# Attention as two 64-row phases with swapped row tiles, single score units between, up heads in the last chunk only

## The chip, the cores and the metric

The kernel runs on one core of one Trainium2 chip. The metric is device time in microseconds, the median of several runs; lower is better.

## The reference

Two stages follow each other. A gated attention without softmax, for eight batches of 3008 rows, 256 columns and 64 columns of z, and then a feed-forward over all 24064 rows:

```python
scores = scale * np.matmul(z, z.transpose(0, 2, 1))   # scale = 1/S, S = 3008
attn = np.maximum(scores, 0.0) ** 2
x = u * np.matmul(attn, v)                            # per batch, [3008, 256]
h = x.reshape(B * S, D) @ w_in                        # d_ff = 2048
g = h * (1.0 / (1.0 + np.exp(-1.702 * h)))
out = g @ w_out
```

Scores are symmetric, since z meets itself.

## The kernel before

**Tiles.** A batch of 3008 rows is 23 blocks of 128 rows and one block of 64; six chunks of 512 columns (the last of 448) are the columns of attention. Everything runs in float16 with float32 sums. ZT holds z transposed, and holds it twice: in partitions 0-63 and again in 64-127.

**Scores.** `scores` (L188) makes a unit: two blocks j of rows for one chunk i. The contraction is over 64 values, so its two matmuls (L198) use the upper and the lower 64 rows of TensorE at once, each into its own PSUM bank of one `sc` tile. ScalarE takes relu and scale out of PSUM (L210, L207), VectorE squares (L224, L215, L208) into an `a` tile. Because of the symmetry a block computed for chunk i also serves, transposed by a DMA on SP's queue (L217, L230: `ad`, `tt`), a later chunk. `take` (L410) pulls the next few units from a fixed list in a planned step of the program; the tables `SCHED`, `SCHED0` (batch 0) and `TAIL` say how many at which step. All units of one `take` issue their matmuls first.

**Attention.** `attend` (L252) makes one chunk's list of steps. For each half c of the 256 columns it sums over j into one PSUM bank `o` (L281), with v (`V`) as the stationary operand, and `a` or `tt` as the moving one. The 23 full blocks use all 128 rows of TensorE; the block of 64 rows is one step (`None`) that runs both halves c at once, one in the upper and one in the lower 64 rows. The halves c follow each other: 23 steps for c = 0, 23 for c = 1, with the half step between or at a place that `AT` or `AT0` gives. In batch 0, chunks 0 and 1, both c run side by side (`both`). At the end of each c `gate` (L286) multiplies the sum by u, transposed, into `xt` on VectorE.

**u.** `load_u` (L161) issues four DMAs from POOL's queue (L168) into one of two `uq` buffers, `turn_u` (L171) transposes on VectorE (L175). In the loop both are issued at the step that `TURN` names, step 12 in most chunks: chunk i of batches 1-7 turns the u of chunk i + 1 and loads that of chunk i + 3 where there is one, batch 0 turns its own chunk i and loads chunk i + 2.

**Feed-forward.** `up_group` (L307) makes two blocks of d_ff for one chunk (L314: `hg`, four matmuls), with the activation on ScalarE (L322) and a scale on VectorE (L323). `down` (L328) makes eight matmuls `yp` of 256 columns (L337), and on every fourth call ScalarE empties the bank (L343) and may issue the output's DMA (L349). The first `LAGY` = 19 up groups of a batch stand between the attention steps of chunks 4 and 5, as `HEAD` says (heads). After attention the rest alternate with `down`; then the last 17 or 19 `down` calls (the tail) carry the first twelve score units of the next batch.

**Buffers and order.** PSUM has two pools: `ps2`, three tiles of two banks (`sc`, `hg`, and `zp` at the start), and `ps1`, two tiles of one bank (`o`, `yp`). All engines run in the written order (`manual_schedule`), so each engine's queue is the order of the Python calls.

```python
for n, step in enumerate(attend(b, i, b == 0 and i < 2, half_at.get(i, 0))):
    ...
    take(b, sched[i].get(n, 0))
    h0, hn = head_at.get(i, (n + 1, 1))
    if head < LAGY and n >= h0 and (n - h0) % hn == 0:
        up_group(b, head)
        head += 1
    step()
```

Of the kernel before, what the change touches and what calls it, by code (L numbers as in the profile page):

```python
# [9 lines left out]
F32 = mybir.dt.float32  # L10
F16 = mybir.dt.float16
P = 128
# [3 lines left out]
def kernel(  # L16
# [20 lines left out]
    NJ = (S + P - 1) // P  # L37
    S0 = (S // P) * P
    SREM = S - S0
    CH = 512  # L40
    NCH = (S + CH - 1) // CH
    CB = CH // P
# [13 lines left out]
    dve, act, pe, sp, pool = nc.vector, nc.scalar, nc.tensor, nc.sync, nc.gpsimd  # L56
# [6 lines left out]
    pu = ctx.enter_context(tc.tile_pool(name="pu", bufs=2))  # L63
    pa = ctx.enter_context(tc.tile_pool(name="pa", bufs=1))
    pw = ctx.enter_context(tc.tile_pool(name="pw", bufs=2))
    ps2 = ctx.enter_context(tc.tile_pool(name="ps2", bufs=3, space=bass.MemoryType.PSUM))
    ps1 = ctx.enter_context(tc.tile_pool(name="ps1", bufs=2, space=bass.MemoryType.PSUM))
    ET = mybir.EngineType
    ctx.enter_context(tc.manual_schedule(engines={ET.PE, ET.Pool, ET.SP, ET.DVE, ET.Activation}))

# [3 lines left out]
    dve.memset(nil, 0.0)  # L74

    ZT, V16, UQ, UT, XT, unit, TT = {}, {}, {}, {}, {}, {}, {}

    def warm_up(n):

        w = ps1.tile([P, CH], F32, name="w", tag="ps1")  # L80
        for k in range(n):
            pe.matmul(w, nil[:, :P], nil, start=(k == 0), stop=(k == n - 1))
# [27 lines left out]

    def first_zt(g):
        z2 = ZT["st"][:, g * CB:(g + 1) * CB]
        zp = ps2.tile([P, CB, P], F16, name="zp", tag="ps2")
        for k in range(CB):
            pe.transpose(zp[:, k, :], z2[:, k, :, :], ident)  # L115
        zt = ZT[0][:, g * CB:(g + 1) * CB, :].rearrange("d n p -> d (n p)")
        nb = CB if g < NCH - 1 else CB - 1
        dst = zt[:, :nb * P].rearrange("d (p n) -> d n p", n=nb)
        if g == 0:
            act.activation(dst, zp[:, :nb, :], AF.Copy, scale=1.0)  # L120
        else:
            dve.tensor_copy(dst, zp[:, :nb, :])  # L122
        if nb < CB:
            dve.tensor_copy(zt[:, nb * P:], zp[:, nb, :])
# [33 lines left out]
    def width(i):  # L158
        return CH if i < NCH - 1 else LAST
# [25 lines left out]
    def folded(b, i):  # L185
        return b > 0 and i < NCH - 1
# [48 lines left out]
    def weights(b, i, j):  # L235

        cj, g = divmod(j, CB)
        n = NCH - 1
        if b == 0 and n in (i, cj):
            return unit[b, i, j // 2][:, j % 2, :width(i)]  # L240
        if i < n and cj == n:
            return TT[b, i, n][:, :, g, :]
        if folded(b, i) and cj == i:
            return unit[b, i, j // 2][:, :, g % 2, :]
        if i == n and cj < n:
            return unit[b, cj, NU - 2 + g // 2][:, g % 2, :LAST]
        if cj >= i:
            return unit[b, i, j // 2][:, j % 2, :width(i)]
        return TT[b, cj, i][:, :, g, :]


    def attend(b, i, both=False, at=0):  # L252


        n = width(i)
        js, cs = list(range(NJ - 1)), range(2)
        own = i * CB
        if b == 0 and i == 3:
            js = js[own:-CB + 1] + js[:own] + js[-CB + 1:]
        elif b and i < NCH - 2:  # L260
            js = js[own:own + 2] + js[own + CB:-CB + 1] + js[own + 2:own + CB] + js[:own] + js[-CB + 1:]
        if both:
            order = [(c, j) for j in js[:-CB] for c in cs] + [(c, j) for c in cs for j in js[-CB:]]
            order.insert(-CB, (None, NJ - 1))
        else:
            order = [(c, j) for c in cs for j in js]
            order.insert(NJ - 1 - at, (None, NJ - 1))
        first = [next(k for k, s in enumerate(order) if s[0] in (c, None)) for c in cs]
        final = [max(k for k, s in enumerate(order) if s[0] in (c, None)) for c in cs]
        acc = {}  # L270

        def step(k):
            half, j = order[k]
            a = weights(b, i, j)
            for c in cs:
                if half not in (c, None):
                    continue
                if k == first[c]:
                    acc[c] = ps1.tile([P, CH], F32, name="o", tag="ps1")
                h = slice(c * SREM, (c + 1) * SREM) if half is None else slice(0, P)  # L280
                pe.matmul(acc[c][:, :n], V16[b][h, j, c, :], a[h], start=k == first[c], stop=k == final[c])  # L281
            for c in cs:
                if k == final[c]:
                    gate(c)

        def gate(c):  # L286
            ut = UT[b, i][:, c].rearrange("p q t -> p (q t)")
            x = XT[b, i]
            if i < NCH - 1 or b % 2:
                dve.tensor_tensor(x[:, c, :n], acc[c][:, :n], ut[:, :n], ALU.mult)  # L290
            else:
                dve.tensor_tensor(x[:, c, :LFULL], acc[c][:, :LFULL], ut[:, :LFULL], ALU.mult)
                dve.tensor_tensor(XT[b + 1, i][:, c, LAST:], acc[c][:, LFULL:n], ut[:, LFULL:n], ALU.mult)

        XT[b, i] = XT.get((b, i)) or pa.tile([P, NCC, CH], F16, name="xt", tag="xt", bufs=8)
        if i == NCH - 1 and b % 2 == 0:
            XT[b + 1, i] = pa.tile([P, NCC, CH], F16, name="xo", tag="xo")
        return [lambda k=k: step(k) for k in range(len(order))]


# [57 lines left out]


    LAGY = 2 * NFG + 3  # L360
    HEAD = {NCH - 2: (14, 4), NCH - 1: (0, 4)}

    def pieces(b, i):

# [6 lines left out]
    def split(lst, sizes):  # L371
# [6 lines left out]

    TAIL = {3: 3, 7: 3, 11: 3, 15: 3}
    SCHED = {
        0: {4: 3, 16: 3, 28: 3, 40: 3},
        1: {8: 3, 23: 3},
        2: {8: 3, 23: 3},
        3: {23: 3},
        4: {8: 3},
        5: {},
    }
    AT = {0: -5, 4: NJ - 1 - 8}  # L390


    TURN = {(True, i): 12 for i in range(1, NCH - 1)}
# [3 lines left out]
    SCHED0 = {  # L397
# [6 lines left out]
    }  # L404
    AT0 = {4: NJ - 1 - 12}
    HEAD0 = {NCH - 2: (28, 4), NCH - 1: (2, 3)}

    queue = []

# [14 lines left out]
    warm_up(9)  # L424
    first_cast(0)
    first_zt(0)
    first_cast(1)
    first_zt(1)
# [7 lines left out]

    for b in range(B):
        nup = NCH * NFG
        sched, head_at, half_at = (SCHED, HEAD, AT) if b else (SCHED0, HEAD0, AT0)
        head = 0  # L440
        for i in range(NCH):
            for n, step in enumerate(attend(b, i, b == 0 and i < 2, half_at.get(i, 0))):
                if b == 0 and i == 0 and n == 5:
                    load_u(0, 0)
                if b == 0 and i == 0 and n in FIRST_ZT:
                    first_zt(FIRST_ZT[n])
                if n == TURN.get((b > 0, i), -1):
                    k = i + (b > 0)
                    turn_u(b, k)
                    if k + 2 < NCH:  # L450
                        load_u(b, k + 2)
                take(b, sched[i].get(n, 0))
                h0, hn = head_at.get(i, (n + 1, 1))
                if head < LAGY and n >= h0 and (n - h0) % hn == 0:
                    up_group(b, head)
                    head += 1
                step()
            if b == 0 and i < NCH - 2:
                hold = const.tile([P, 1], F16, name=f"hold{i}")
                pool.tensor_copy(hold, XT[b, i][:, 0, :1])  # L460
                if i < 2:
                    w1v = moe_w_in.rearrange("(q k c) f -> q c k f", k=NCC, c=QW)
                    for k in range(2 * i, 2 * i + 2):
                        pool.dma_start(W1[k * QW:(k + 1) * QW], w1v[k])
                elif i == NCH - 3:
                    pool.dma_start(W2, moe_w_out.rearrange("(fo p) c -> p fo c", p=P))
        more = b + 1 < B
        if more:
            for i in range(2):
                load_u(b + 1, i)  # L470
            load_z(b + 1)
            for n0 in range(0, NJ, VB):
                load_v(b + 1, n0, sp)
            fill(b + 1)
        downs = down_list(b)
        for q in range(head, nup):
            if more and q in (head + 14, head + 20):
                k = int(q == head + 20)
                turn_u(b + 1, k)
                load_u(b + 1, k + 2)  # L480
            up_group(b, q)
            if q >= LAGY:
                down(b, *downs.pop(0))
        for n in range(len(downs)):
            if more:
                take(b + 1, TAIL.get(n, 0))
            down(b, *downs[n])
# [30 lines left out]
```

## Time and profile before

| | before |
|---|---|
| median of three runs | 1251.93 us (1250.12 to 1258.75) |
| profiled execution, its own time | 1250.78 us |
| its span | 1248.8 us |
| PE busy | 1239.4 us (99%) |
| ACT, DVE, POOL busy | 754.2, 628.5, 233.3 us |
| granted TensorE clock | 1.00 |

The span runs from the first to the last instruction in the profile; the execution's own time has a little more around it. A row of the profile gives line, engine, operation, the tile written and those read, shapes, count, busy time and the mean of one. PEld is the loading of stationary operands, which overlaps the matmuls of PE. A matmul's row is longer than the distance to the next one, since they are pipelined: the distance of two starts is what one costs. "Idle before" is the engine's idle time ahead of an instruction, with what ended it.

### The profile page before, as it was taken

How to read it: one execution, taken by the hardware profiler on the slowest of the kernel's cores; microseconds unless marked ns; L12 is line 12 of the kernel's file. 1: busy time of each engine (PE TensorE's matmuls, PEld its weight loads, DVE VectorE, ACT ScalarE, POOL GpSimd, SP SyncE). 2: the span in 40 equal slices, each digit the busy share in tenths (PEclk: the TensorE clock that was granted, in tenths of full speed). 3: DMA queues.
4: the chain of work that ended last, by engine and by line, in shares of the span. 5: the costliest groups of instructions: out<-in, count | busy, mean ns of one | idle time of the engine just before them, and what ended most of it. 6: DMA issues, size and time to landing. Idle time of an engine off the chain costs nothing.

```text
span 1248.8 us, 19199 instructions
## 1 busy us (share of the span) xinstructions
PE 1239.4 (99%) x7575; PEld 682.6 (55%) x7575; DVE 628.5 (50%) x901; ACT 754.2 (60%) x829; POOL 233.3 (19%) x333
## 2 busy tenths in 40 slices
PE   8999999999999999999999999999999999999998
PEld 3345764466544675446754467444674446734566
DVE  7665445544455445554454544655445454464431
ACT  5776674566745667366673666745666456664663
POOL 4224202221022210223102230022211222000000
PEclk9999999999999999999999999999999999999999
DMA  9937279622886228852397524965239552493001
GB/s 229 185 66 171 71 167 181 126 68 69 186 167 127 69 85 191 162 106 68 95 192 155 106 76 99 205 130 107 98 102 197 120 113 84 117 196 74 1 35 68
DMA packets 370394, 151.75 MB, mean 122 GB/s; under 512 B 312864, under 2 KB 363936, under 8 KB 370304
## 3 DMA queue, kind: packets, MB, share of 16 engines
q1 hardware_dynamic: 311840, 96.38, 36.3%
q0 software_dynamic: 33440, 29.37, 12.0%
q10 hardware_dynamic: 25024, 24.78, 6.0%
q8 instruction: 59, 0.97, 0.3%
q14 instruction: 31, 0.25, 0.1%
HBM read 60.29 MB, written 24.64 MB: 68 GB/s over the span
## 4 chain that ended last, share of the span: by engine, by line
PE 97%; DVE 1%; issue 1%; ACT 1%; DMA 0%; SPq 0%; ACTq 0%; DVEq 0%
PE o L281 38%; PE yp L337 27%; PE hg L314 26%; PE sc L198 6%; DVE a L224 1%; ACT rl L210 0%; DMA zf<-in_z_dram 0%; DVE zst L109 0%; DVE ut L175 0%; DVE xt L290 0%; DVE ZT L122 0%; PE zp L115 0%; ACT y L343 0%; SPq L95 0%; ACTq L210 0%
## 5 line engine op out<-in xcount | busy, mean ns | idle before, releaser
L322 ACT ACTIVATE gf<-hg 128x1024 f32<-128x1024 f32 (+1 forms) x384 | 385.9, 1006 | 232.4 <-PE hg L314 221.5
L323 DVE TENSOR_SCALAR gt<-gf 128x1024 f16<-128x1024 f32 (+1 forms) x384 | 278.1, 725 | 326.7 <-ACT gf L322 324.4
L210 ACT ACTIVATE rl<-sc 128x1024 f16<-128x1024 f32 x311 | 299.5, 1025 | 161.2 <-PE sc L198 160.0
L337 PE MATMUL yp<-W,gt 128*128 128x256 f16 x3008 | 371.1, 273 | 0.0
L281 PEld LDWEIGHTS <-V 128*128 128x128 f16 (+1 forms) x2304 | 213.1, 98 | 280.0 <-issue 43.3
L314 PE MATMUL hg<-xt,W 128*128 128x512 f16 (+1 forms) x1408 | 354.6, 374 | 0.0
L337 PEld LDWEIGHTS <-gt 128*128 128x128 f16 x3008 | 292.1, 98 | 90.6 <-issue 11.1
L281 PE MATMUL o<-a,V 128*128 128x512 f16 (+2 forms) x1244 | 297.0, 373 | 0.8 <-DVE a L224 0.8
L224 DVE TENSOR_TENSOR a<-rl 128x1024 f16<-128x1024 f16 x276 | 192.2, 697 | 170.3 <-ACT rl L210 170.2
L168 POOL DMA_DIRECT2D uq<-in_u_dram x188 | 126.1, 678 | 629.0 <-DVE ut L175 619.3
L281 PE MATMUL o<-tt,V 128*128 128x512 f16 x920 | 219.0, 379 | 0.9 <-DVE xt L290 0.9
L314 PEld LDWEIGHTS <-W 128*128 128x128 f16 x1536 | 149.7, 98 | 125.6 <-issue 1.4
L153 POOL CAST V<-vst 128x512 f16<-128x512 f32 x96 | 67.9, 746 | 143.8 <-PE o L281 116.1
L198 PE MATMUL sc<-ZT 64*128 64x512 f16 (+1 forms) x692 | 93.4, 373 | 0.9 <-DVE ZT L122 0.8
L343 ACT ACTIVATE y<-yp 128x512 f32<-128x512 f32 x96 | 56.4, 588 | 50.8 <-PE yp L337 50.3
L290 DVE TENSOR_TENSOR xt<-o,ut 128x512 f16<-128x512 f32 x80 | 54.7, 685 | 36.7 <-PE o L281 36.7
L175 DVE STREAM_TRANSPOSE ut<-uq 128x1024 f32<-128x1024 f32 (+1 forms) x48 | 58.4, 1216 | 0.2
L198 PEld LDWEIGHTS <-ZT 64*128 64x128 f16 x692 | 24.1, 94 | 58.3 <-issue 45.7
L215 DVE TENSOR_TENSOR a<-rl 128x1024 f16<-128x1024 f16 x35 | 24.2, 692 | 45.2 <-ACT rl L210 44.9
L207 ACT ACTIVATE rl<-sc 128x512 f16<-128x512 f32 x35 | 20.9, 597 | 41.6 <-PE sc L198 41.6
L281 PE MATMUL o<-ad,V 128*128 128x512 f16 x140 | 41.6, 379 | 0.0
L314 PE MATMUL hg<-xo,W 128*128 128x512 f16 x128 | 32.8, 379 | 0.0
(28 smaller groups left out, 92.3 us busy)
## 6 DMA issues: line engine op xcount, KB each, us to landing
out_dram<-y ACTq DMA_DIRECT2D x40, 512.0 KB, 2.9
vst<-in_v_dram SPq DMA_DIRECT2D x39, 512.0 KB, 4.5
uq<-in_u_dram POOLq DMA_DIRECT2D x156, 128.0 KB, 2.9
tt<-a SPq DMA_TRANSPOSE x230, 3.2
uq<-in_u_dram POOLq DMA_DIRECT2D x32, 112.0 KB, 3.1
vst<-in_v_dram SPq DMA_DIRECT2D x8, 384.0 KB, 4.4
out_dram<-y ACTq DMA_DIRECT2D x7, 384.0 KB, 3.1
zst<-in_z_dram POOLq DMA_DIRECT2D x7, 368.0 KB, 6.0
```

The lines of the kernel that those rows point to most:

```text
L153: pool.tensor_copy(V16[b][:, n0:n0 + VB, k, :].rearrange("p n (q c) -> p n q c", c=QW), vst.rearrange("p n (q k c) -> p n q k c", k=NCC, c ...
L168: eng.dma_start(uq[k * QW:(k + 1) * QW, :n // QW].rearrange("t q k c -> t q (k c)"), src[:, :, cs])
L175: dve.transpose(ut[:, :, :n // QW, :].rearrange("p k q t -> p q k t"), UQ.pop((b, i))[:, :n // QW])
L198: pe.matmul(sc[:, r, :m * P], zt[h, 2 * kp + r, :], zt[h, (qi + 1) * CB - m:(qi + 1) * CB, :], start=True, stop=True,)
L210: act.activation(rl, sc, AF.Relu, scale=csc)
L224: dve.tensor_tensor(a, rl, rl, ALU.mult)
L281: pe.matmul(acc[c][:, :n], V16[b][h, j, c, :], a[h], start=k == first[c], stop=k == final[c])
L314: pe.matmul(hg[:, e, :n], W1[:, c, ff * P:(ff + 1) * P], XT[b, i][:, c, :n], start=(c == 0), stop=(c == NCC - 1),)
L322: act.activation(gf[:, :, :n], hg[:, :, :n], AF.Gelu_apprx_sigmoid, scale=1.0 / FSC)
L323: dve.tensor_scalar(g, gf[:, :, :n], FSC, None, ALU.mult)
L337: pe.matmul(yp[:, s % 2, :], GT[b, k, ff // CB][:, ff % CB, s * P:(s + 1) * P], W2[:, ff, :], start=(ff == 0), stop=(ff == NFF - 1),)
L343: act.activation(Y[b, k][:, s0:s + 1, :], yp[:, :s % 2 + 1, :], AF.Copy, scale=1.0 / FSC)
```

## The change

Three things change together.

- **Row mode.** In chunks 0 to 4 (in batch 0: 2 to 4) every attention step is a pair of 64-row matmuls. In phase one the upper 64 rows of block j feed c = 0 and the lower 64 rows feed c = 1; in phase two they are swapped, so that each c gets both halves of each block. The block of 64 rows is one pair between the phases. Both sums are open over the whole chunk, and both gates stand at its end. As the row tiles change banks between the phases, a `nop` on POOL waits for the last pair of phase one (`post`), and the first pair of phase two waits for it (`behind`). Chunk 5 keeps the full mode, with its half step moved to the front.
- **Score units.** The tables now place units one by one between attention steps, with two at step 24 (`NJ`), behind the last pair of phase one; the tail takes two units at six places instead of three at four.
- **Heads and PSUM.** All 19 heads stand in chunk 5, spread over it. `ps2` has two tiles instead of three, `ps1` four instead of two, and the first ZT tiles (`zp`) use `ps1`.

```diff
-    ps2 = ctx.enter_context(tc.tile_pool(name="ps2", bufs=3, space=bass.MemoryType.PSUM))
-    ps1 = ctx.enter_context(tc.tile_pool(name="ps1", bufs=2, space=bass.MemoryType.PSUM))
+    ps2 = ctx.enter_context(tc.tile_pool(name="ps2", bufs=2, space=bass.MemoryType.PSUM))
+    ps1 = ctx.enter_context(tc.tile_pool(name="ps1", bufs=4, space=bass.MemoryType.PSUM))
...
+    SYNC = mybir.DependencyInfo(mybir.DependencyClass.Sync, mybir.DependencyReason.DATA)
+    TOP, LOW, FULL = slice(0, SREM), slice(SREM, P), slice(0, P)
+
+    def post(last):
+
+        sig = pool.nop()
+        for m in last:
+            tc.add_manual_dep(sig.ins, m.ins.name, SYNC, reason="row tiles of one bank")
+        return sig
+
+    def behind(sig, m):
+        tc.add_manual_dep(m.ins, sig.ins.name, SYNC, reason="row tiles of one bank")
...
+        half = [(0, TOP, NJ - 1), (1, LOW, NJ - 1)]
         if both:
-            order = [(c, j) for j in js[:-CB] for c in cs] + [(c, j) for c in cs for j in js[-CB:]]
-            order.insert(-CB, (None, NJ - 1))
+            order = [[(c, FULL, j)] for j in js[:-CB] for c in cs] + [[(c, FULL, j)] for c in cs for j in js[-CB:]]
+            order.insert(-CB, half)
+        elif i == NCH - 1:
+            order = [half] + [[(c, FULL, j)] for c in cs for j in js]
         else:
-            order = [(c, j) for c in cs for j in js]
-            order.insert(NJ - 1 - at, (None, NJ - 1))
...
+            order = [[(0, TOP, j), (1, LOW, j)] for j in js] + [half] + [[(1, TOP, j), (0, LOW, j)] for j in js]
...
+            done = []
+            for m in order[k]:
+                c, h, j = m
+                if (k, m) == first[c]:
+                    acc[c] = ps1.tile([P, CH], F32, name="o", tag="ps1")
+                ins = pe.matmul(
+                    acc[c][:, :n], V16[b][h, j, c, :], weights(b, i, j)[h],
+                    start=(k, m) == first[c], stop=(k, m) == final[c],
+                )
+                if k == turn:
+                    behind(acc["sig"], ins)
+                done.append(ins)
+            if k == turn - 1:
+                acc["sig"] = post(done)
...
-    HEAD = {NCH - 2: (14, 4), NCH - 1: (0, 4)}
+    HEAD = 2
...
-    TAIL = {3: 3, 7: 3, 11: 3, 15: 3}
+    TAIL = {n: 2 for n in (2, 5, 7, 10, 13, 16)}
     SCHED = {
-        0: {4: 3, 16: 3, 28: 3, 40: 3},
-        1: {8: 3, 23: 3},
-        2: {8: 3, 23: 3},
-        3: {23: 3},
-        4: {8: 3},
+        0: {n: 1 for n in (1, 4, 7, 11, 28, 30, 33, 36, 39, 43)} | {NJ: 2},
+        1: {n: 1 for n in (4, 9, 34, 40)} | {NJ: 2},
+        2: {n: 1 for n in (4, 9, 34, 40)} | {NJ: 2},
+        3: {n: 1 for n in (38,)} | {NJ: 2},
+        4: {n: 1 for n in (2,)} | {NJ: 2},
         5: {},
     }
-    AT = {0: -5, 4: NJ - 1 - 8}
...
     SCHED0 = {
         0: {0: 1, 6: 2, 14: 2, 22: 2, 30: 2, 38: 2},
         1: {0: 2, 8: 2, 15: 2, 22: 2, 30: 2, 38: 2},
-        2: {0: 2, 8: 2, 23: 3, 34: 3},
-        3: {8: 3, 23: 3},
-        4: {1: 3, 12: 3, 23: 3},
+        2: {n: 1 for n in (0, 3, 7, 11, 30, 34, 38, 42)} | {NJ: 2},
+        3: {n: 1 for n in (4, 9, 34, 40)} | {NJ: 2},
+        4: {n: 1 for n in (0, 3, 6, 9, 12, 32, 36)} | {NJ: 2},
         5: {0: 1},
     }
...
-                h0, hn = head_at.get(i, (n + 1, 1))
-                if head < LAGY and n >= h0 and (n - h0) % hn == 0:
+                if i == NCH - 1 and n >= HEAD and (n - HEAD) * LAGY // (2 * NJ - 2 - HEAD) >= head and head < LAGY:
                     up_group(b, head)
```

More of the change, by code (lines that the diff above doesn't have):

```diff
@@ L112, in first_zt @@
         z2 = ZT["st"][:, g * CB:(g + 1) * CB]
-        zp = ps2.tile([P, CB, P], F16, name="zp", tag="ps2")
+        zp = ps1.tile([P, CB, P], F16, name="zp", tag="ps1")
         for k in range(CB):
@@ L249, in weights, with attend @@
         return TT[b, cj, i][:, :, g, :]
-    def attend(b, i, both=False, at=0):
+    def attend(b, i, both=False):
         n = width(i)
@@ L261, in attend @@
             js = js[own:own + 2] + js[own + CB:-CB + 1] + js[own + 2:own + CB] + js[:own] + js[-CB + 1:]
+        half = [(0, TOP, NJ - 1), (1, LOW, NJ - 1)]
         if both:
-            order = [(c, j) for j in js[:-CB] for c in cs] + [(c, j) for c in cs for j in js[-CB:]]
-            order.insert(-CB, (None, NJ - 1))
-        else:
-            order = [(c, j) for c in cs for j in js]
-            order.insert(NJ - 1 - at, (None, NJ - 1))
-        first = [next(k for k, s in enumerate(order) if s[0] in (c, None)) for c in cs]
@@ L269, in attend @@
-        final = [max(k for k, s in enumerate(order) if s[0] in (c, None)) for c in cs]
-        acc = {}
-        def step(k):
-            half, j = order[k]
-            a = weights(b, i, j)
-            for c in cs:
[L276 to L283, printed above, removed]
+            order = [[(c, FULL, j)] for j in js[:-CB] for c in cs] + [[(c, FULL, j)] for c in cs for j in js[-CB:]]
@@ new lines, in attend @@
+            order.insert(-CB, half)
+        elif i == NCH - 1:
+            order = [half] + [[(c, FULL, j)] for c in cs for j in js]
+        else:
+            order = [[(0, TOP, j), (1, LOW, j)] for j in js] + [half] + [[(1, TOP, j), (0, LOW, j)] for j in js]
+        flat = [(k, m) for k, ms in enumerate(order) for m in ms]
+        first = {c: next(m for m in flat if m[1][0] == c) for c in cs}
+        final = {c: [m for m in flat if m[1][0] == c][-1] for c in cs}
+        acc, turn = {}, NJ if order[-1][0][1] != FULL else -1
@@ new lines, in step @@
+        def step(k):
+            done = []
[12 more added lines that the diff above has]
+                acc["sig"] = post(done)
+            for c in cs:
+                if k == final[c][0]:
@@ L399 @@
         1: {0: 2, 8: 2, 15: 2, 22: 2, 30: 2, 38: 2},
[3 rows of a table removed]
+        2: {n: 1 for n in (0, 3, 7, 11, 30, 34, 38, 42)} | {NJ: 2},
+        3: {n: 1 for n in (4, 9, 34, 40)} | {NJ: 2},
+        4: {n: 1 for n in (0, 3, 6, 9, 12, 32, 36)} | {NJ: 2},
         5: {0: 1},
     }
-    AT0 = {4: NJ - 1 - 12}
-    HEAD0 = {NCH - 2: (28, 4), NCH - 1: (2, 3)}
     queue = []
@@ L438 @@
         nup = NCH * NFG
-        sched, head_at, half_at = (SCHED, HEAD, AT) if b else (SCHED0, HEAD0, AT0)
+        sched = SCHED if b else SCHED0
         head = 0
         for i in range(NCH):
-            for n, step in enumerate(attend(b, i, b == 0 and i < 2, half_at.get(i, 0))):
+            for n, step in enumerate(attend(b, i, b == 0 and i < 2)):
                 if b == 0 and i == 0 and n == 5:
```

## The prediction

> **What bounds the kernel now.** I read the page's busy line and the chain first, then the timeline of PE, where the price of the changed thing can be read off start times.
>
> ```profile
> span 1248.8 us, 19199 instructions
> PE 1239.4 (99%) x7575; PEld 682.6 (55%) x7575; DVE 628.5 (50%) x901; ACT 754.2 (60%) x829; POOL 233.3 (19%) x333
> PE 97%; DVE 1%; issue 1%; ACT 1%; DMA 0%; SPq 0%; ACTq 0%; DVEq 0%
> ```
>
> TensorE is the chain from end to end, so any time that PE gains or stands is worth its full length. But a busy PE is not a PE at its peak. The timeline of PE (start, length, line, operation) shows what it pays:
>
> ```profile
> 303.45 1.04 PE L337 MATMUL yp<-W,gt 128*128 128x256 f16 x8
> 304.32 1.03 PE L314 MATMUL hg<-xo,W 128*128 128x512 f16 x4
> 305.18 1.04 PE L337 MATMUL yp<-W,gt 128*128 128x256 f16 x8
> ...
> 316.49 0.82 PE L198 MATMUL sc<-ZT 64*128 64x512 f16 x6
> 317.25 3.67 PE L337 MATMUL yp<-W,gt 128*128 128x256 f16 x32
> 320.85 0.82 PE L198 MATMUL sc<-ZT 64*128 64x512 f16 x6
> 321.60 3.67 PE L337 MATMUL yp<-W,gt 128*128 128x256 f16 x32
> 325.20 0.61 PE L198 MATMUL sc<-ZT 64*128 64x512 f16 x4
> ```
>
> Eight yp take 304.32-303.45 = 0.87, or 0.109 each; four hg of 512 columns take 0.86, or 0.216 each. A period of 32 yp and three score pairs is 4.355 (mean of two). Work in it: 32 x 0.109 + 3 x 0.216 = 4.14, since the two 64-row matmuls of a pair start 3-4 ns apart in the records and a pair costs 0.216 like one full matmul. The remaining 0.215 is the price of one run of 64-row work in a 128-row stream, both switches together. The program has 131 such runs: 28 us of the span.
>
> The second thing to see is the chain behind a row of u (chunk 1 of a batch), on three engines:
>
> ```profile
> 344.65 0.82 PE L198 MATMUL sc<-ZT 64*128 64x512 f16 x6
> 345.08 2.86 ACT L210 ACTIVATE rl<-sc 128x1024 f16<-128x1024 f32 x3 [1.56 <-PE sc L198]
> 346.14 0.69 DVE L224 TENSOR_TENSOR a<-rl 128x1024 f16<-128x1024 f16 x1 [1.45 <-ACT rl L210]
> ...
> 347.97 0.69 DVE L224 TENSOR_TENSOR a<-rl 128x1024 f16<-128x1024 f16 x1 [0.23 <-ACT rl L210]
> 348.58 1.24 DVE L175 STREAM_TRANSPOSE ut<-uq 128x1024 f32<-128x1024 f32 x1
> ...
> 350.11 2.62 POOL L168 DMA_DIRECT2D uq<-in_u_dram  x4 [18.46 <-DVE ut L175]
> ```
>
> Score to ACT 0.43, ACT to its square on DVE 1.06, squares 0.92 apart, transpose 0.08 before the square's end, then the four u issues on POOL 0.29 after it. And how far POOL's queue looks ahead, from its instructions of line 168 in the next chunk:
>
> ```profile
> L168 POOL DMA_DIRECT2D uq<-in_u_dram x4: 632/634/635, 362.0 to 363.8; - x4
> L168 POOLq EVENT_SEMAPHORE  x2: 43/43/43, 363.4 to 363.4; - x2
> ```
>
> The two semaphore instructions stand behind all four issues in the program, and run at 363.4, just after the third started (363.2). So one issue is queued ahead, and what stands behind four issues runs some 1.55 + 0.12 = 1.68 after the transpose ends (1.67 to 1.71 in the three chunks of this batch).
>
> **What the skill says.** TensorEngine Tiling (Array Packing), Key Properties: changing the tiling mode drains TensorE, changing only the tile doesn't. The trace agrees: 0.215 for in and out. TensorE: Matmul & The Clock Gate, Part 3: matmuls of different row groups run together, about 4 ns apart; here 3-4 ns. The first page's Gotcha 1: different row tiles must not write one PSUM bank at a time; no run here shows the breach, but it is why the change swaps banks behind a signal. PSUM — Partial Sum Buffer, Engine vs sequencer instructions: a nop belongs to the sequencer, which waits only until what stands before it is dispatched. The 363.4 agrees, with the limit that the fourth issue is dispatched only when the third starts.
>
> **The change, step by step.** All against the profiled execution: span 1248.8, time 1250.78, so 2.0 outside it; it lies 1.15 below the median 1251.93.
>
> 1. Fewer runs. Attention of chunks 0-4 becomes one 64-row stream with the scores inside it. In the changed program's order I count 65 runs for 131 (TAIL has six instead of four per batch, each batch's chunks 0-4 are one). 66 x 0.215 = -14.2. Matmul work is unchanged: 47 pairs replace 46 full matmuls and one pair.
>
> 2. Pairs in a long stream. The 128-row o matmuls become pairs with two weight loads each. Nearest evidence: four pairs in a row (three sc, one o) keep 0.216, only the pair just after the switch takes 0.227. An instruction then comes every 54 ns, as in the yp stream, which PE keeps up. I take 0; the other end is 0.011 for each of 1750 pairs, +19.
>
> 3. The turn. After phase one a nop on POOL waits for the last pair; the weight load of phase two waits for the nop. Two score units stand between (2 x 0.216), and a signal takes about 0.05 each way: pair ends at +0.38, nop done at +0.5, before phase two is due at +0.65. 38 turns; for 22 I take 0 (0 to 0.1 each).
>  But in chunks 1 and 2 of batches 1-7 and chunks 2 and 3 of batch 0 the nop stands behind the four u issues of step 12. They wait for the transpose, that for the square of the last unit before step 12, at step 9. From that unit's score: 0.43 + 1.06 + 0.69 - 0.08 + 1.24 + 1.68 + 0.04 (the nop) + 0.05 = 5.1. Phase two is due 18 slots of 0.216 later (that unit, steps 9-23, two units): 3.9. PE stands 1.2; behind it stands all of phase two. In batch 0, chunk 2, the last unit is at step 11: 16 slots, 3.45, so 1.65. Together 15 x 1.22 + 1.65 = +20.0. Bounds: 1.0 to 1.6 each (POOL's second and third issue are now and then 0.5 late), 16 to 26.
>
> 4. Two score buffers instead of three. A unit's matmul now waits for ACT's relu of the unit two before, and ACT takes 1.02, 0.92 apart when queued. At the turn of chunk 0 units A, B go out at 0.22 and 0.43; the next are at steps 28, 30, 33, 36, 39, 43. C is due at 1.51, A's relu ends at 0.22+0.43+1.02 = 1.67: 0.2 lost; D two steps on, against B's: 0.27; then every three steps and a unit, 0.86, against 0.92: 3 x 0.05. 0.63 x 7 = +4.4.
>  At the start of chunk 0 ACT is still behind, for the y of the last down and its DMA come between:
>
> ```profile
> 320.95 0.60 ACT L343 ACTIVATE y<-yp 128x512 f32<-128x512 f32 x1 [1.01 <-PE yp L337]
> 321.58 0.38 ACTq L349 DMA_DIRECT2D out_dram<-y  x1
> 322.06 1.02 ACT L210 ACTIVATE rl<-sc 128x1024 f16<-128x1024 f32 x1 [0.51 <-PE sc L198]
> ```
>
>  They hold ACT for 1.1. After an even batch (46 downs) the last two TAIL units come one down before the end; from their score: relus at 0.43 and 1.35, y 2.26, relu of unit one at 3.33, done 4.35; unit three (step 7) is due at 3.36: 1.05 lost, four times. After an odd batch two more downs give time: 0.43, three times. +5.5. The ring together +9.9 (6 to 13).
>
> 5. Batch 0, chunk 5. The half step now comes first and needs the square of the unit scored just before it: 0.43 + 1.06 + 0.69 + 0.05, less its own slot: +2.0. Later batches score it in chunk 4.
>
> 6. At nothing: up heads only in chunk 5 (2 or 3 steps of 0.19 and four hg are 1.24 or more per head, ACT needs 1.02 and the buffer is back after 2.1 of 2.48); both gates at a chunk's end (four ps1 buffers hide them; otherwise 1.4 per chunk); ZT copies in ps1; SP's transposes, same number and order, some a few us later: those of units 10 and 11 of chunk 1 start about 8 steps later, land about 5 before their step 20. Without that slack each late us would count.
>
> Sum: -14.2 + 20.0 + 9.9 + 2.0 = +17.7; 1266.5 span, **1268.5** measured, 1.3% above the median. One per cent (12.5) is about what this measurement tells from no change.
>
> **Rivals.**
> - The nop is not held by the issues (POOL runs its semaphore instructions as soon as the first issue is released: 3.7 from the score, under 3.9). For it: the skill's sentence on dispatch. Against: the 363.4. Then the 20.0 is gone: 1248.5, not slower. It decides below 0.15 of hold behind the transpose instead of 1.68.
> - As that, and the ring has slack as well (ACT 60% busy): 1250.8 - 14.2 + 2.0 = 1238.6, faster. Against: in chunk 0 the units come closer than ACT's 0.92.
> - Turns stand but the ring doesn't: 1258.6.
> - Pairs hold 0.227 in a long stream: 1268.5 + 19 = 1287.7. Against: the third and fourth pairs of the records.
>
> **How the numbers follow.** Forecast 0.58, nop not held 0.17, both gone 0.05, ring alone gone 0.10, slow pairs 0.10. The forecast's own range from steps 3 and 4 is 1260 to 1281; 1246 to 1283 takes in the first and third rivals. Slower by over 1% (above 1264.4): 0.58 of it less a sixth for its low end, and slow pairs, 0.58; faster 0.06; the rest 0.36.
>
> **What would show it.** The waits should gain PE weight loads of o on POOL, 16 of them over 1 us, and sc on ACT rl, about 7 x 6 and 7 of half to one us. PE's timeline should show 64-row pairs 0.216 apart in attention. If no wait on POOL's nop stands, step 3 is wrong; if pairs are wider, step 2; if sc waits for nothing, step 4.

## The result, and the profile after

| | before | after |
|---|---|---|
| median | 1251.03 us (1249.97 to 1258.75, 4 runs) | 1268.97 us (1267.02 to 1273.41, 4 runs) |
| ratio to before | | 1.0138, 95% interval 1.0094 to 1.0182 |
| profiled execution, span | 1248.8 us | 1271.6 us |

The change is 1.4% slower. Predicted were 1268.5 us. The profiled execution of after is its slowest (1273.41 us); the spans of the other three are 1265.2, 1265.4 and 1268.9. So its trace holds some microseconds that the median doesn't.

The page of after, the span, TensorE's row, and the chain:

```profile
span 1271.6 us, 22720 instructions
PE 1232.6 (97%) x9323; PEld 698.7 (55%) x9323; DVE 621.9 (49%) x901; ACT 762.3 (60%) x829; POOL 233.4 (18%) x333
PE 91%; ACT 2%; DVE 2%; DMA 2%; issue 2%; POOL 2%; ACTq 0%; DVEq 0%; SPq 0%
```

PE was 97% of the chain and is 91%. The chain follows a wait back through the work that ended it, so the other 9% are more than the time that PE stood. How long it stood is in the answer on PE's waits of after (engine, line, what it waited for; microseconds in all, times, longest). The first three rows were not there before, and the fourth was 0.8, at the start:

```profile
PE o L294 <- POOLq L83: 17.7, 15, 1.7
PE sc L211 <- ACT rl L223: 4.7, 8, 0.9
PE o L294 <- DMA tt<-a: 4.3, 1, 4.3
PE o L294 <- DVE a L237: 4.1, 2, 2.2
```

The ends of matmuls are modelled and reach into the gaps, so these figures are low. I measure each gap from start to start, less the matmuls' own time.

**The turn.** The timeline of after, chunk 1 of batch 1 (start, length, engine, line, operation, count, and idle time before it with its releaser), and the empty instruction's semaphore behind the loads:

```profile
200.18 1.24 DVE L188 STREAM_TRANSPOSE ut<-uq 128x1024 f32<-128x1024 f32 x1
200.67 1.04 PE L294 MATMUL o<-tt,V 64*128 64x512 f16 x8
201.53 0.61 PE L211 MATMUL sc<-ZT 64*128 64x512 f16 x4
201.71 2.57 POOL L181 DMA_DIRECT2D uq<-in_u_dram  x4 [47.35 <-PE o L294]
203.16 1.84 PEld L294 LDWEIGHTS <-V 64*128 64x128 f16 x20 [1.51 <-POOLq L83]
...
L83 POOLq EVENT_SEMAPHORE  x1: 17/17/17, 203.1 to 203.1; - x1
```

The last pair of phase one and two score units are done with by 201.53 + 2 x 0.216 = 201.96. Phase two starts at 203.16: 1.20 lost. The transpose of u ended at 201.42 and the semaphore of the empty instruction (L83) ran at 203.1, 1.68 later, behind four issues of which the third had just started. From start to start I find 15 such gaps, 1.20 to 1.83 us, 20.3 us in all. The sixteenth place (batch 0, chunk 3) shows none. A longer wait came just before it, and in two traces below without that wait (an earlier turn, units spaced) the gap stands there, 1.18.

**The two score buffers.** The timeline of after at the start of chunk 0, batch 1:

```profile
183.30 0.60 PE L294 MATMUL o<-a,V 64*128 64x512 f16 x4
183.53 1.02 ACT L223 ACTIVATE rl<-sc 128x1024 f16<-128x1024 f32 x1 [0.52 <-DVE a L237]
184.61 0.39 PE L211 MATMUL sc<-ZT 64*128 64x512 f16 x2 [0.71 <-ACT rl L223]
185.90 1.69 PE L294 MATMUL o<-a,V 64*128 64x512 f16 x14
187.41 0.61 PE L294 MATMUL o<-ad,V 64*128 64x512 f16 x4
```

The unit's matmul was due at 183.30 + 2 x 0.216 = 183.73 and started when the relu of the unit two before ended: 0.88 lost. Such gaps of 0.87 to 0.94 (after even batches) and 0.44 to 0.46 (after odd ones), with 0.21, 0.27 and three of 0.05 behind the turn of each chunk 0, make 9.4 us. The last two rows show the pairs: seven in 187.41 - 185.90 = 1.51, 0.216 each.

**Batch 0.** Two things, the first foreseen, the second not. The half step of chunk 5 waits for a unit that was scored just before it, and in chunk 3 PE waits for a transposed tile:

```profile
86.90 0.38 PE L211 MATMUL sc<-ZT 64*128 64x512 f16 x2
89.12 0.66 PE L294 MATMUL o<-a,V 64*128 64x448 f16 x3 [1.84 <-DVE a L237]
...
59.68 1.67 PE L294 MATMUL o<-tt,V 64*128 64x512 f16 x14
65.63 1.89 PE L294 MATMUL o<-tt,V 64*128 64x512 f16 x8 [4.28 <-DMA tt<-a]
67.31 1.83 PE L294 MATMUL o<-a,V 64*128 64x512 f16 x8
```

89.12 - 86.90 - 0.216 = 2.0. In chunk 3, 65.63 - 59.68 - 7 x 0.216 = 4.44, and then four pairs take 67.31 - 65.63 = 1.68, 0.42 each: TensorE came back at half speed for eight pairs, 1.6 us more. The answers for the tile `tt` from 28 to 60 us show what was late: how long a transpose takes to land.

Before:

```profile
DMA to landing us min/median/max: 2.8/4.9/8.0
```

After:

```profile
DMA to landing us min/median/max: 3.0/8.1/17.0
```

This second wait does not come with every execution. Two experiments below (an earlier turn, units spaced) leave batch 0 as it is in after; their traces show at most 12.8 and 13.1 us to landing, no wait in chunk 3, only one of 0.42 and one of 0.61 at the start of chunk 2, and no pairs at half speed. So the 6.0 us (4.4 and 1.6) are not a fixed price of the change.

### The profile page after: what moved, and what is told of

Same layout as the page of the kernel before. It is cut to its first block, busy times and chain, and to the rows that moved or that the text cites. A ratio compares the mean times of both kernels' runs of the same rounds, so it can differ in the third digit from the quotient of the medians.

```text
span 1271.6 us, 22720 instructions
## 1 busy us (share of the span) xinstructions
PE 1232.6 (97%) x9323; PEld 698.7 (55%) x9323; DVE 621.9 (49%) x901; ACT 762.3 (60%) x829; POOL 233.4 (18%) x333
## 4 chain that ended last, share of the span: by engine, by line
PE 91%; ACT 2%; DVE 2%; DMA 2%; issue 2%; POOL 2%; ACTq 0%; DVEq 0%; SPq 0%
PE o L294 34%; PE yp L358 26%; PE hg L335 26%; PE sc L211 5%; ACT rl L223 2%; POOL uq L181 2%; DMA tt<-a 1%; DVE ut L188 1%; DVE a L237 0%; DVE zst L122 0%; DMA zf<-in_z_dram 0%; ACT y L364 0%; ACTq L370 0%; DVE ZT L135 0%; DVE xt L311 0%
## 5 line engine op out<-in xcount | busy, mean ns | idle before, releaser
L223 ACT ACTIVATE rl<-sc 128x1024 f16<-128x1024 f32 x311 | 305.5, 1026 | 265.3 <-PE sc L211 258.9
L344 DVE TENSOR_SCALAR gt<-gf 128x1024 f16<-128x1024 f32 (+1 forms) x384 | 272.3, 710 | 298.8 <-ACT gf L343 297.2
L294 PEld LDWEIGHTS <-V 64*128 64x128 f16 (+1 forms) x4052 | 224.6, 95 | 287.6 <-POOLq L83 28.3
L294 PE MATMUL o<-a,V 64*128 64x512 f16 (+2 forms) x2010 | 318.8, 374 | 20.3 <-POOLq L83 16.2
L294 PE MATMUL o<-tt,V 64*128 64x512 f16 (+1 forms) x1762 | 211.1, 377 | 5.7 <-DMA tt<-a 4.3
L211 PE MATMUL sc<-ZT 64*128 64x512 f16 (+1 forms) x692 | 114.8, 369 | 5.7 <-ACT rl L223 4.7
L166 POOL CAST V<-vst 128x512 f16<-128x512 f32 x96 | 70.6, 771 | 134.1 <-PE o L294 102.3
L211 PEld LDWEIGHTS <-ZT 64*128 64x128 f16 x692 | 35.0, 94 | 57.1 <-issue 27.9
L311 DVE TENSOR_TENSOR xt<-o,ut 128x512 f16<-128x512 f32 x80 | 51.4, 684 | 19.7 <-PE o L294 19.7
L294 PE MATMUL o<-ad,V 64*128 64x512 f16 x280 | 42.8, 376 | 0.0
L220 ACT ACTIVATE rl<-sc 128x512 f16<-128x512 f32 x35 | 21.3, 607 | 10.2 <-PE sc L211 10.2
```

What stands on the lines that cost most here:

```text
L166: pool.tensor_copy(V16[b][:, n0:n0 + VB, k, :].rearrange("p n (q c) -> p n q c", c=QW), vst.rearrange("p n (q k c) -> p n q k c", k=NCC, c ...
L211: pe.matmul(sc[:, r, :m * P], zt[h, 2 * kp + r, :], zt[h, (qi + 1) * CB - m:(qi + 1) * CB, :], start=True, stop=True,)
L223: act.activation(rl, sc, AF.Relu, scale=csc)
L294: ins = pe.matmul(acc[c][:, :n], V16[b][h, j, c, :], weights(b, i, j)[h], start=(k, m) == first[c], stop=(k, m) == final[c],)
L344: dve.tensor_scalar(g, gf[:, :, :n], FSC, None, ALU.mult)
```

## The experiments

Each time is the median of a kernel's runs; ratios are to the kernel before on the same chip, with the 95% interval. The kernel before took 1249.9, 1250.7 and 1250.5 us in the three groups below. Edits are to the changed kernel unless another is named. The interval of the changed kernel itself is 0.4% either way, some 5 us, so a gain against its 1268.97 is known no better than that from the times; the traces, which show the waits themselves, are sharper. But each trace is one execution, and not always a typical one.

### First group: the parts of the loss, one by one

**The loads behind the empty instruction.** The transpose of u stays at its step, the four issues go behind the turn.

```diff
...
-                    if k + 2 < NCH:
-                        load_u(b, k + 2)
+                    later = k + 2 if k + 2 < NCH else None
+                    if later and not (n < NJ and (b or i > 1) and i < NCH - 1):
+                        load_u(b, later)
+                        later = None
...
+                if n == NJ and later:
+                    load_u(b, later)
+                    later = None
```

> The only edit: the four u issues of step 12 stand behind the nop in POOL's queue instead of ahead of it (the transpose stays at step 12). Theory (the nop is held by the issues): the 16 long waits of PE for POOL go, 20 us less than the changed kernel, about 1248 to 1250. Rival (the turn costs as such: signal to POOL and back, the swap of row tiles): the waits stay near 1.2 us and the time near 1268.

Measured: 1254.56 us, ratio 1.0045 (1.0031 to 1.006), 14 less than the changed kernel and some 5 more than expected. Of the waits on POOL none is left, but there are more waits for DMAs than in after. PE's waits in this kernel:

```profile
PE o L294 <- DMA tt<-a: 5.8, 2, 4.6
PE o L294 <- DMA ad<-a: 3.5, 3, 2.4
```

The first row is batch 0 (1.30 and 4.79, with 1.5 for seven pairs at half speed behind the longer one). The second is new: in four batches (from start to start 0.91, 0.59, 0.23 and 2.54), always at step 6 of chunk 3, for `ad`, the transposed copy of the chunk's own unit. So the stall at the turn is gone as step 3 said, and part of it came back at once as another wait.

**An earlier turn.** The turn of batches 1 to 7 at step 8 instead of 12, before the unit of step 9.

```diff
-    TURN = {(True, i): 12 for i in range(1, NCH - 1)}
+    TURN = {(True, i): 8 for i in range(1, NCH - 1)}
```

> The only edit: transpose and u issues of batches 1-7 at step 8 instead of 12, that is ahead of the score unit of step 9; the issues still stand ahead of the nop. Theory (the chain score unit, relu, square, transpose, issues, nop is what is late): the chain now starts from the unit of step 4, 24 slots of 0.216 = 5.18 us before phase two is due, against 5.1 us of chain: 14 waits shrink from 1.25 to about 0 to 0.1, 16 to 17.5 us less than the changed kernel, about 1251. Rival (only the place behind the issues counts, whenever they are issued): no change, 1268.

Measured: 1255.39 us, ratio 1.0036 (1.002 to 1.0052). Twelve of the fourteen gaps in batches 1 to 7 are gone, two of 0.5 are left, and batch 0, where nothing was moved, keeps its 1.62 and 1.18. One wait of 1.48 for an `ad` came. The median is 4 us more than expected. The profiled execution, at 1250.98, is the fastest of ten, so what the others have on top is not in its trace. Since the loads are only issued earlier, not moved across the empty instruction, the two edits agree: it is the time at which POOL comes to the empty instruction that counts.

**Units of chunk 0 spaced.** The table of chunk 0 gives ACT time between units.

```diff
-        0: {n: 1 for n in (1, 4, 7, 11, 28, 30, 33, 36, 39, 43)} | {NJ: 2},
+        0: {n: 1 for n in (1, 4, 12, 15, 18, 29, 33, 37, 41, 45)} | {NJ: 2},
```

> The only edit: the score units of chunk 0 in batches 1-7 at steps 1, 4, 12, 15, 18, 24 (two), 29, 33, 37, 41, 45 instead of 1, 4, 7, 11, 24 (two), 28, 30, 33, 36, 39, 43. Theory (with two score buffers PE waits for ACT where units come closer than ACT's 0.92 us): the waits of sc for relu in chunk 0 go, about 9 us less than the changed kernel, 1259. Rival (the two buffers cost nothing, the difference lies elsewhere): within 2 us of 1268.

Measured: 1258.98 us, ratio 1.0069 (1.0054 to 1.0084). All waits of sc on ACT in batches 1 to 7 are gone, and those at the turn are as they were:

```profile
PE o L294 <- POOLq L83: 18.8, 16, 1.7
```

The gain, 1268.97 - 1258.98 = 10.0, fits step 4's 9.9 within what the times can tell; that all those waits are gone is the surer sign. At this spacing two buffers cost nothing. One wait of 1.30 for an `ad` came, in batch 3.

**Three repairs together.** Loads behind, chunk 0 spaced, and the unit that chunk 5 of batch 0 waited for taken in chunk 4.

```diff
-        4: {n: 1 for n in (0, 3, 6, 9, 12, 32, 36)} | {NJ: 2},
-        5: {0: 1},
+        4: {n: 1 for n in (0, 3, 6, 9, 12, 32, 36, 40)} | {NJ: 2},
+        5: {},
```

> Three edits on the changed kernel: the u issues behind the nop, the units of chunk 0 spaced, and the last unit of batch 0 scored at step 40 of chunk 4 instead of at step 0 of chunk 5, where the half step needs it at once. Theory (independent terms): 20.0 + 9.3 + 2.0 us less, about 1237, faster than the kernel before by 1.1%. Rival (pairs of 64 rows in a long stream, or a new late transpose, cost something that these terms hide): over 1243.

Measured: 1250.31 us, ratio 0.9999 (0.9982 to 1.0015). The expectation failed by 13 us. The waits on POOL and on ACT are gone, the wait on the unit of chunk 5 fell from 2.0 to 0.50, but the time is not what it should be. The profiled execution, 1255.48 us, is the slowest of twelve. PE's waits in it:

```profile
PE o L294 <- DMA ad<-a: 9.0, 7, 3.1
PE o L294 <- DMA tt<-a: 7.9, 3, 5.7
```

The timeline of this kernel at chunk 3 of batch 7 shows the first kind at its longest:

```profile
1123.09 6.38 SPq L243 DMA_TRANSPOSE tt<-a  x4
...
1125.91 0.51 PE L211 MATMUL sc<-ZT 64*128 64x512 f16 x4
1126.35 1.02 ACT L223 ACTIVATE rl<-sc 128x1024 f16<-128x1024 f32 x1 [3.73 <-PE sc L211]
1127.40 0.69 DVE L228 TENSOR_TENSOR a<-rl 128x1024 f16<-128x1024 f16 x1 [2.91 <-ACT rl L223]
...
1129.57 1.30 SPq L230 DMA_TRANSPOSE ad<-a  x1
...
1136.18 0.61 PE L294 MATMUL o<-ad,V 64*128 64x512 f16 x4 [3.07 <-DMA ad<-a]
```

The unit is scored at step 24 of chunk 2 (before: at step 8) and squared 2.2 us later. SP is still busy with four transposes queued earlier and issues this one at 1129.57; it lands 6.6 us later (the own units of chunk 3 in this kernel: 4.1 to 6.6). PE reaches step 6 of chunk 3 at 1132.93, 7.02 after the scoring, and stands 3.25. The same place in after:

```profile
1145.86 0.49 PE L211 MATMUL sc<-ZT 64*128 64x512 f16 x4
...
1148.10 1.19 SPq L230 DMA_TRANSPOSE ad<-a  x1
...
1154.18 0.59 PE L294 MATMUL o<-ad,V 64*128 64x512 f16 x4
```

There the stall of the turn in chunk 2, 1.29 to 1.83 us, lies between the scoring and the use, so PE comes 8.3 to 8.9 after the scoring. But the tile is also earlier: in the seven batches of after it is there 5.3 to 6.8 us after the scoring, in the three repairs 7.6 to 10.2. So in after's trace it would have been in time without the stall as well. That a stall can hide a late tile shows in the trace with units spaced, which keeps the turn's stall: in two batches the tile was there 7.12 and 8.05 after the scoring and PE did not wait, in one 9.57, and it waited 1.30. The margin is thin, and the tile comes later once the stalls are gone; how much of that is the closer order of the transposes and how much the moved loads is not shown here.

### Second group: is that the cause, and what do switches cost

**The empty instruction on ScalarE.**

```diff
-        sig = pool.nop()
+        sig = act.nop()
```

> The changed kernel with the empty instruction of the turn on ScalarE's queue instead of POOL's; the u loads stay where they are. Theory (the empty instruction runs late only because it is queued behind four load issues on POOL): the same 15 waits of 1.2 to 1.8 us at the turn go, about 20 us, without any move of a load; what came out in their place when the loads were moved (4 us for the own transposed unit of chunk 3, 2 to 3 us more in batch 0) comes out here too, so 1253 to 1256 us. Rival (the turn costs its 1.3 us in itself, by the semaphore or by the swap of row tiles, whichever engine signals): no change, 1267 to 1270 us.

Measured: 1249.47 us, ratio 0.9999 (0.9984 to 1.0013). One word takes 19.5 us off 1268.97, and no load moves. The timeline of this kernel, at the same turn as above:

```profile
194.54 0.61 PE L211 MATMUL sc<-ZT 64*128 64x512 f16 x4
194.71 2.57 POOL L181 DMA_DIRECT2D uq<-in_u_dram  x4 [47.34 <-DVE ut L188]
194.82 1.99 PEld L294 LDWEIGHTS <-V 64*128 64x128 f16 x20 [0.17 <-ACTq L83]
194.97 2.34 PE L294 MATMUL o<-a,V 64*128 64x512 f16 x20
```

194.54 + 2 x 0.216 = 194.97: nothing lost. No turn of this trace loses more than 0.1. The semaphore and the swap cost nothing measurable in themselves, which rules out the rival. The median is 3.5 us below the range that I expected: of the waits for DMAs only one for `ad` (2.17, with 1.7 for pairs at half speed after it) and one in batch 0 (1.83) came out in the profiled execution, fewer than with the loads moved. The chunk's own unit of chunk 3 was there 5.8 to 7.0 us after its scoring in six batches and 9.2 in one; with the loads moved behind the turn it took 6.6 to 9.5.

**Single units in the kernel before.** 128-row streams, three score buffers and the old heads, with the changed kernel's tables of units; the half step moves to place 24, right behind the two units there (`AT`, `AT0`, not shown).

```diff
-    TAIL = {3: 3, 7: 3, 11: 3, 15: 3}
+    TAIL = {n: 2 for n in (2, 5, 7, 10, 13, 16)}
     SCHED = {
-        0: {4: 3, 16: 3, 28: 3, 40: 3},
-        1: {8: 3, 23: 3},
+        0: {n: 1 for n in (1, 4, 7, 11, 28, 30, 33, 36, 39, 43)} | {NJ: 2},
+        1: {n: 1 for n in (4, 9, 34, 40)} | {NJ: 2},
...
```

> The kernel before (128-row streams, three score buffers, its up heads) with only the score units spread as in the changed kernel's tables: one unit at a time. Theory (a switch of TensorE between 128-row and 64-row work costs 0.19 to 0.215 us per return trip): 263 isolated stretches of 64-row work instead of 131, so +132 x 0.19 to 0.215 = +25 to +28 us on 1250, 1275 to 1279 us, with no long waits. Rival (the switches are free or hidden, and the changed kernel's loss comes from single units): either no change, about 1251 us, or waits for score buffers of some 10 us as in the changed kernel.

Measured: 1277.96 us in one run, span 1276.0, so 27.2 more than before. 27.2 / 132 = 0.206 per stretch, inside the expected 0.19 to 0.215, and there are no long waits. Its timeline, with two units in a stream of yp, gives the price again:

```profile
325.66 0.60 PE L198 MATMUL sc<-ZT 64*128 64x512 f16 x4
326.20 2.79 PE L337 MATMUL yp<-W,gt 128*128 128x256 f16 x24
328.92 0.60 PE L198 MATMUL sc<-ZT 64*128 64x512 f16 x4
```

A period is 3.26; 24 yp of 0.109 and two pairs of 0.216 are 3.05; 0.21 is the return trip between the modes. So single units pay 0.21 each unless the stream around them is in 64-row mode too.

**Chunk 3's own unit first.** The three repairs, and in `pieces`, for batches 1 to 7:

```diff
+        if i == NCH - 3:
+            return [lst[k] for k in (0, 4, 5, 1, 2, 3)]
         k = max(len(lst) - 6, 0)
         return lst[:k] + lst[-2:] + lst[k:-2]
```

> All three repairs together (loads behind the empty instruction, chunk 0's units respaced, batch 0's last unit moved into chunk 4) and in batches 1 to 7 chunk 3's own unit scored at step 4 of chunk 2 instead of step 24. Theory (the repairs' gain of 30 us was taken back by that unit's transposed copy being late, about 10 us over the batches, and by two late transposes in batch 0, about 9 us): the seven waits of 0.6 to 3.3 us in chunk 3 go, 1240 to 1242 us; batch 0's two waits stay. Rival (SP's queue of transposes is full as a whole, so the same lateness comes out at the next tile): other waits for transposed tiles of the same sum, 1249 to 1251 us.

Measured: 1242.64 us, ratio 0.9916 (0.9888 to 0.9945), within a microsecond of the expected range. No wait for an `ad` is left; PE's waits show only batch 0:

```profile
PE o L294 <- DMA tt<-a: 7.7, 2, 6.7
```

So the rival, another tile late in its place, is out: the other transposes had room for it, only that unit was given too little time.

**W1 late in batch 0.** As chunk 3's own unit first, and:

```diff
-                if i < 2:
+                if i >= 2:
                     w1v = moe_w_in.rearrange("(q k c) f -> q c k f", k=NCC, c=QW)
-                    for k in range(2 * i, 2 * i + 2):
+                    for k in range(2 * i - 4, 2 * i - 2):
                         pool.dma_start(W1[k * QW:(k + 1) * QW], w1v[k])
-                elif i == NCH - 3:
+                if i == NCH - 3:
```

> As the one with chunk 3's own unit first, and in batch 0 W1's four quarters are loaded after chunks 2 and 3 instead of after chunks 0 and 1 (they are used from chunk 5 on). Theory (in batch 0 the transposes land up to 15 us after their issue because W1's copies share the DMA engines with them between 30 and 60 us): batch 0's waits of 1.2 and 5.9 us and the slow clock after them (about 1.9 us) go, 8 to 9 us less than the version without this edit, 1231 to 1233 us. Rival (the transposes are late by their own number, or because of u's loads and SP's queue): the wait at chunk 3 of batch 0 stays, the two versions are within 2 us of each other.

Measured: 1235.56 us, ratio 0.9877 (0.9859 to 0.9895), 7.1 less than without the edit (four runs each, so the gain is known to a few microseconds), 1.2% faster than before, and some 3 above the expected range. Batch 0 has no wait for a DMA, and the transposes of `tt` between 28 and 60 us land in time. The answers for this tile, first without the edit, then with it:

```profile
DMA to landing us min/median/max: 5.2/13.0/15.7
```

```profile
DMA to landing us min/median/max: 2.7/5.2/7.5
```

So with W1's copies out of the way the transposes are in time; that they were late by sharing the DMA engines is argued, not shown. The other traces agree: in the nine with W1 early the longest landing in this stretch is 8.0 (before) to 17.0 (after), in the two of the changed order with W1 late 7.3 and 7.5. In the profiled execution waits for transposed tiles of 0.3 to 1.2 us in four later batches, 3.4 us together, take a part of it back.

### Third group: a control, and a version without moved loads

**The kernel before with W1 late.** All four quarters after chunk 2 (its first head stands in chunk 4).

```diff
-                if i < 2:
+                if i == 2:
...
-                    for k in range(2 * i, 2 * i + 2):
+                    for k in range(4):
...
```

> The kernel before with one edit: in batch 0 all four quarters of W1 are loaded after chunk 2 instead of two after chunk 0 and two after chunk 1. It is the control for the version with W1 late. Theory (W1's place costs only where a transposed tile is awaited; the kernel before has no such wait in its trace): no change, 1248 to 1252 us. Rival (W1's early place slows batch 0 in itself, so part of the 7 us was to be had without the change): 1242 to 1246 us.

Measured: 1250.38 us, ratio 0.9986 (0.9964 to 1.0008): no change. So the gain from W1's place is not one that the kernel before had left lying; late transposes cost time only where PE waits for them, and the trace of the kernel before shows no such wait in batch 0.

**All repairs, the empty instruction on ScalarE.** As with W1 late, but with `act.nop()` and the loads where the change has them.

> As the one with W1 late, but the turn's empty instruction is on ScalarE's queue and the u loads stay ahead of it, instead of being moved behind it. Theory (what the loads need is only to be out of the way of the empty instruction): the same, 1233 to 1237 us, no waits at the turn. Rival (the loads at step 12 collide with transposes that are due soon, which moving them behind the turn avoided): up to 5 us slower with more waits for transposed tiles; or the remaining 3.4 us of such waits go with the earlier loads, 1231 to 1233 us.

Measured: 1235.49 us, ratio 0.9876 (0.9851 to 0.9902): the same time as with the loads moved. Its trace has no wait for a transposed tile, where the version with the loads moved had 3.4 us of them, but the medians don't differ. The profiled execution's page, span and chain:

```profile
span 1232.9 us, 22720 instructions
PE o L294 39%; PE yp L358 27%; PE hg L335 26%; PE sc L211 6%; DMA zf<-in_z_dram 0%; DVE a L237 0%; DVE zst L122 0%; DVE ZT L135 0%; ACT rl L223 0%; PE zp L128 0%; ACT y L364 0%; SPq L108 0%
```

Matmuls are 98% of the chain. This is the simpler of the two fastest kernels, 15 us below before.

## Why the prediction was right, and where not

| step | predicted | trace of after, start to start | by experiment |
|---|---|---|---|
| 1, fewer 64-row stretches | -14.2 | 131 to 65 stretches | 0.206 each by single units, 66 of them -13.6 |
| 2, pairs in a long stream | 0 | 0.216 each | |
| 3, the turn | +20.0 | +20.3 | -19.5 with the word `act` |
| 4, two score buffers | +9.9 | +9.4 | -10.0 with chunk 0 spaced |
| 5, batch 0, chunk 5 | +2.0 | +2.0 | 0.5 is left when scored earlier, not timed alone |
| 6, SP's transposes and the rest | 0 | +6.0 in the profiled execution | 20.4 in the trace of the three repairs, its slowest execution |

**Steps 1 to 5 held**, each at its size. What carried step 3 is one line of the profile of before: a semaphore instruction behind four issues that ran when the third had started. In after the same 1.68 stands between transpose and semaphore. Two of the 15 gaps, 1.80 and 1.83, lie above the bound of 1.6. The rival that POOL would run ahead needed, by the prediction's own sum, a hold below 1.68 - 1.22 = 0.46; the 0.15 that it names does not follow from its terms, and 1.68 is far from both. In step 4 the loss at the start of chunk 0 comes to 4.35 - 3.36 = 0.99 and not 1.05 by its own figures; 0.87 to 0.94 were measured. The rival of the score buffers, 1258.6 if the turns stand alone, is what spacing chunk 0 gave: 1258.98. And the first rival's 1248.5, the nop not held, is near what ScalarE's queue gave: 1249.47.

**Step 6 held only in part.** The prediction put SP's transposes at nothing, since their number and order stay and the two that it looked at, units 10 and 11 of chunk 1, had five microseconds to spare. It looked at the wrong unit. Chunk 3's own unit moved from step 8 to step 24 of chunk 2, and PE comes to its transposed copy, at step 6 of chunk 3, 7.02 us after the scoring, plus what it stood between. Score to square takes 2.2 of that, so 4.8 are left for SP's queue and a landing, 3.1 to 4.5 us long in after and 4.1 to 6.6 in the three repairs. In the changed kernel as it is, the stall of step 3 widens the 4.8 to 6 or more, and no batch of after waits for this tile. In batch 0 the transposes landed up to 17.0 us after their issue, and the profiled execution lost 4.4, and 1.6 for the pairs at half speed; the spans of the other three executions, 2.7 to 6.4 shorter, and the two traces with the same batch 0 suggest that this is not in every execution.

So the total of 1268.5 was right for the reasons given. That it met the median within half a microsecond is luck: the four executions run from 1267.02 to 1273.41. And the ledger was not one of independent items. The prediction's second rival, both stalls gone, was given 1238.6, and with both and most of step 5 gone the kernel took 1250.31. The missing term came out when the stalls were taken away, in the trace of that kernel: 10.1 for `ad` (seven waits of 0.65 to 3.25), 8.4 for `tt` and 1.9 for the pairs at half speed behind the longest. With it repaired as well, the kernel takes 1235.5, 15.0 less than before. That is close to step 1, but not step 1 alone: the kernel before stands 0.50, 0.38 and 0.50 us for the gates of chunks 0 and 1 of batch 0, and with four `ps1` buffers these 1.4 are gone; 66 return trips at 0.206 are 13.6.

**Open.** W1 is as early in the kernel before, and there the transposes land within 8.0 us. It need not be the order: at 31.2 us, where both kernels have issued the same DMAs in the same sequence, the transpose issued beside W1's first copies took 7.3 us to land before and 10.4 after, and in the kernel before with single units, whose chunks 0 and 1 of batch 0 have the same units, 11.5. Why it varies was not tried. Nor was why moving the loads behind the turn gave 1254.56 where ScalarE's queue gave 1249.47; in the first the own unit of chunk 3 is later and there are more DMA waits, in one execution each.

## What to carry to other kernels

A signal is only as early as the queue it stands in: put it on an engine that has nothing slow ahead of it, and count every DMA issue that POOL has to start before it. A stall gives time to everything produced before it and used after it, so before adding up what repairs would bring, list each transfer whose slack shrank and see what is left of it without the stall. And a change that moves production later needs the check of slack for each unit that is used next, the one with the nearest use first.

## What the runs showed of the hardware

- Transposes by DMA in the same stretch of the program landed 2.8 to 8.0 us after their issue in the trace of before and 3.0 to 17.0 in that of after, and SP's queue stood up to 9.4 us on the issue of one (after, 28 to 60 us):

```profile
L243 SPq DMA_TRANSPOSE tt<-a x11: 1234/2085/9440, 27.3 to 58.1; - x11
```

- After PE had waited 4.4 us (after), eight pairs ran at 0.42 instead of 0.216; after 4.8 us (loads moved) seven, after 5.9 us (three repairs) nine, after 6.8 us (own unit first) ten, so 1.5 to 2.1 us on top. The length of the wait doesn't settle it: a wait of 3.25 us (three repairs) left the pairs behind it at full speed, and one of 2.17 us (the empty instruction on ScalarE) was followed, 1.4 us later, by seven pairs at half speed.
- Two 64-row matmuls with two weight loads keep 0.216 per pair over whole chunks, with both sums open in two banks, and a swap of row tiles behind a signal costs nothing measurable if the signal is in time.
